# Turning the second chunk's y by VectorE blocks and placing transfers instead of TensorE transposes, in a one-core mixer kernel

## The chip, the cores and the metric

The kernel runs on one core of one Trainium2 chip. The metric is the device time of one execution in microseconds (us). Before the change it is 747.01 us, the median of 3 runs (746.77 to 747.2).

## The reference, cut to what matters

```python
def _layernorm(x, axis=-1, eps=1e-5):
    m = jnp.mean(x, axis=axis, keepdims=True)
    v = jnp.var(x, axis=axis, keepdims=True)
    return (x - m) / jnp.sqrt(v + eps)
...
    x = A_x                                   # [1, 2048, 512]
    xn = _layernorm(x, axis=-1)
    s = _A_ref(xn, A_wqkv, A_wo)              # 32 heads of 16, causal window of 256, then @ wo
    g = _silu(_B_ref(xn, B_w1, B_b1, B_w2, B_b2))
    return x + s * g
...
def _B_ref(x, w1, b1, w2, b2):                # w1 [512, 1792], w2 [1792, 512]
    y = _layernorm(x, axis=-1)
    h = _gelu(jnp.einsum("bsd,df->bsf", y, w1) + b1)
    return jnp.einsum("bsf,fd->bsd", h, w2) + b2
```

The MLP's input `y` is thus the layernorm of `xn`, itself a layernorm.

## The kernel before, in words

All products are made in three passes: each operand is split into a high part (a cast) and a low part (the rest), and high x high, high x low and low x high are summed. `split` (line 69) makes the pair: ScalarE casts the high part, VectorE subtracts it for the low part.

Tokens are worked in four chunks of 512. The attention comes first, up to about 433 us of the profiled span, with an order that is written out by hand (steps `t`, lists `plan`, `fills`, `ends`). The layernorms `xn` of the first two chunks are kept in DRAM (`xn_d`), the attention's raw outputs and the denominators of its softmax in `oT_d`.

Then the MLP and the output projection follow, chunk by chunk. The loop at line 1087 works chunk 0 (`c == 0`) and chunk 1 (`c == 1`). Its inner loop (line 1112) has 15 steps `i`; a step handles one block `f` of 128 hidden features:

- `activate(f)`: ScalarE makes the gelu `g` and the high part `gh`, VectorE the low part `gl`. `gh` and `gl` have two buffers each.
- `project(f)` of the block before it: 12 matmuls into the four accumulators `acc`, in the order high, high, low for each of them.
- `hidden(f)`: 12 matmuls `h` with the transposed `y` as moving operand. In chunk 0 only blocks 4 and 5 are made in the loop, at steps 2 and 3; the others were made during the attention and, from block 6 on, lie in DRAM (`h_d`), from where they are fetched as `hr`. The blocks are worked in the order 2, 3, 0, 1, 4, 5, 6 to 13.

Between these the loop of chunk 0 does three side jobs:

- `late_w`: the rest of the weights (`w`, `wos`) is split.
- The denominators: `fetch_sums` (step 2) loads `den` from `oT_d`; VectorE takes its reciprocal in four parts at steps 4 to 7; SyncE writes it to `rden_d`. At steps 8 to 11 `load_o` loads the attention's outputs `or` and, spread over partitions, their reciprocals `w<-rden_d`; a step later VectorE multiplies them (line 1149), and another step later `split_o` makes `ohl`, which the output projection reads.
- The second chunk's `y`: `load_y(1)` at step 4 loads four tiles of 128 tokens from `xn_d`; from step 6 to 11 VectorE makes mean and variance (`BATCH_NORM`), GpSimd the power -1/2 (`rs`), and VectorE applies them.

`end_chunk` (line 944) is the seam between two chunks: VectorE adds the bias to `acc`, ScalarE makes the silu, and for each of four tiles TensorE makes the output projection `s` (12 matmuls), VectorE multiplies it by the gate, GpSimd adds `x` (`xo`), SyncE stores. Before tiles 0 and 2 of the seam after chunk 0, `between` calls `y_transpose` twice (line 643): for each 128 features TensorE turns four 128x128 blocks of `y` into a PSUM bank `yt`, and `split` makes high and low part of the turned `y` from it (`yh`, `xnT`). After the seam chunk 1 begins with three `hidden`, which read these.

The `y` of chunks 2 and 3 goes another way already, during chunk 1: ScalarE normalises, VectorE turns each tile in square blocks of 32x32 in place (`turn_y`, line 888), SyncE stores it to `z_d`, and `fetch_y` (line 895) loads it back in four transfers for each 128 features, which put the blocks in their places.

The order on each engine is the program's order: every operation is issued through the class `Ordered` (line 32). Only SyncE, which issues all the DMAs, is left to the scheduler where `nc.sync.on` is False; in the loop it was on for chunk 1 and off for chunk 0 (line 1111). An engine works its instructions in order, so one that waits holds up all behind it on that engine.

Of the kernel before, what the change touches and what calls it, by code (L numbers as in the profile page):

```python
# [9 lines left out]
F32 = mybir.dt.float32  # L10
# [8 lines left out]
P = 128  # L19
NCH = S // 512  # L20
NKB = S // P
KT = D // P
# [28 lines left out]
def mixer_kernel(ctx, tc, x, wqk, wv, wo, w1, b1, w2, b2, out):  # L51


    nc = SimpleNamespace(**{name: Ordered(tc, name) for name in ("tensor", "vector", "scalar", "gpsimd", "sync")})
# [5 lines left out]
    dram = ctx.enter_context(tc.tile_pool(name="dram", bufs=1, space=bass.MemoryType.DRAM))  # L60
# [8 lines left out]
    def split(dst_hi, dst_lo, src, eng=None):  # L69

        (eng or nc.scalar.copy)(dst_hi, src)
        nc.vector.tensor_sub(dst_lo, src, dst_hi.bitcast(F32))
# [4 lines left out]
    def load(pool, tag, src, name, shape=(P, 512)):  # L77
        t = pool.tile(list(shape), F32, tag=tag, name=name)
        nc.sync.dma_start(t, src)
        return t  # L80
# [83 lines left out]
    def load_x(c, pools, name):  # L164
        return [load(*pools[i % len(pools)], x[512 * c + P * i: 512 * c + P * (i + 1), :], f"{name}_{c}_{i}")
                for i in range(4)]
# [15 lines left out]
    xn_d = dram.tile([8, P, D], F32, name="xn_d")  # L182
# [3 lines left out]
    w_d = {"w1": dram.tile([P, NF * 512], F32, name="w1_d"), "w2": dram.tile([P, NF * 512], F32, name="w2_d"),  # L186
           "wo": dram.tile([P, 4 * 512], F32, name="wo_d")}
    g_d = dram.tile([NF, P, 512], F32, name="g_d")
    z_d = dram.tile([2, 4, P, 512], F32, name="z_d")
    mT_d = dram.tile([NQ, NCH, 32, P], F32, name="mT_d")  # L190


# [31 lines left out]
    ident = const.tile([P, P], F32, name="ident")  # L224
# [360 lines left out]
    mlp = {}  # L585
# [34 lines left out]
    def w_part(kind, a, f):  # L620
        return {"w1": w1_part, "w2": w2_part, "wo": lambda a, f: wos[:, a, f]}[kind](a, f)
# [6 lines left out]
    def fetch(kind, f):  # L628

        nc.sync.dma_start(w_part(kind, 1, f).bitcast(F32), w_d[kind][:, 512 * f: 512 * (f + 1)])  # L630
# [9 lines left out]
    def y_steps(a, b):  # L640
        run(mlp["ln"][a:b])

    def y_transpose(c, kt, ps=None):
        ts = mlp["y"]
        if ps is None:
            ps = ps_yt.tile([P, 512], F32, tag="b", name=f"yt_{c}_{kt}")
        for i in range(4):
            nc.tensor.transpose(ps[:, P * i: P * (i + 1)], ts[i][:, P * kt: P * (kt + 1)], ident)
        split(mlp["yy"][0][kt], mlp["yy"][1][kt], ps)

    def hidden_mm(ps, f, k):
        kt, (a, b) = k // 3, PASSES[k % 3]
        nc.tensor.matmul(ps, w1_part(a, f)[:, P * kt: P * (kt + 1)], mlp["yy"][b][kt],
# [38 lines left out]
    ln = layernorm(xs[0], "A0", True, True, 3)  # L692
# [171 lines left out]
    ps_yt = ctx.enter_context(tc.tile_pool(name="ps_yt", bufs=2, space=PSUM))  # L864
# [6 lines left out]
    wos = cp.tile([P, 2, 4, 512], F32R, name="wos")  # L871
    for f in range(W2_FIRST, NF):
        fetch("w2", f)
    for f in range(6, NF, 2):
        t = gp.tile([P, 2, 512], F32, tag="ohl", name=f"hr_{f}", bufs=4)
        nc.sync.dma_start(t, h_d[f - 6: f - 4].rearrange("f p t -> p f t"))
        ready.update({f: t[:, 0], f + 1: t[:, 1]})
# [3 lines left out]
        fetch("wo", g)  # L881

    def load_y(c):
        if c > 1:
            return load_x(c, ((mlp["yp"], "y"),), "y")
        return [load(mlp["yp"], "y", xn_d[4 * c + i], f"y_{c}_{i}") for i in range(4)]

    def turn_y(c, tiles):

        for i in tiles:  # L890
            y = mlp["y"][i]
            nc.vector.transpose(y, y)
            nc.sync.dma_start(z_d[c - 2, i], y)

    def fetch_y(c, kt, dst):

        for k in range(4):
            at = z_d[c - 2, 0, 0, 128 * kt + 32 * k: 128 * kt + 32 * k + 32]
            nc.sync.dma_start(dst[32 * k: 32 * k + 32].rearrange("p (t j) -> p t j", j=32),
                              bass.AP(tensor=at.tensor, offset=at.offset, ap=[[512, 32], [32 * 512, 16], [1, 32]]))  # L900

# [185 lines left out]
    for c in range(2):  # L1087
        accs = open_accs(c)
        gs, os_, hs, wanted = {}, [], {}, []
        made = ready if c == 0 else {}  # L1090

        def hidden(f):
            hs[f] = (ps_yt if c and f % 2 else ps_st).tile([P, 512], F32, tag="b", name=f"h_{c}_{f}")
            for k in range(3 * KT):
                hidden_mm(hs[f], f, k)

        def activate(f):
            if f in made and f in soon:
                gs[f] = made[f]
                return  # L1100
            src = made[f] if f in made else hs.pop(f)
            g = src if f in made and f < 2 else t2.tile([P, 512], F32, tag="t2", name=f"g_{c}_{f}")
            nc.scalar.activation(g, src, AF.Gelu_apprx_tanh, bias=b1s[:, f: f + 1])
            gs[f] = split_g(c, f, g, nc.scalar.copy)

        order = [2, 3, 0, 1, 4, 5, *range(6, NF)] if c == 0 else [*range(NF)]
        ahead = 2 + c
        for f in range(ahead if c else 0):
            hidden(f)
        o_from, o_late = (0, 0) if c else (8, 1)  # L1110
        nc.sync.on = c > 0
        for i in range(NF + 1):
            if i < NF:
                activate(order[i])
            if c and i in (1, 2, 6, 7):
                y_steps(6, 10)
            if c and i >= 10 and i < 14:
                second_y(i - 10)
            if c and i == 14:
                kept["w"] = bigp.tile([P, 768], F32R, tag="wb1", name="wsh")  # L1120
                combine_w(0)
            if c == 0:
                for kind, f in late_w[LATE[i]: LATE[i + 1]]:
                    settle(kind, f, nc.scalar.copy, nc.vector)
            if i >= 1:
                project(accs, [(order[i - 1], gs.pop(order[i - 1]))], order[0], order[-1])
            if i + ahead < NF and order[i + ahead] not in made and order[i + ahead] > 1:
                hidden(order[i + ahead])
            if c == 0:
                if i == 2:  # L1130
                    den = fetch_sums()
                if 4 <= i < 8:
                    nc.vector.reciprocal(den[:, P * (i - 4): P * (i - 3)], den[:, P * (i - 4): P * (i - 3)])
                    if i == 7:
                        nc.sync.dma_start(rden_d.rearrange("g a (c t) -> (g a c) t", c=NCH), den)
                if i == 4:
                    mlp["y"] = load_y(1)
                if i == 6:
                    mlp["ln"] = layernorm(mlp["y"], "C1", False)
                for back, (a, b) in enumerate(((0, 2), (2, 4), (4, 5), (5, 6), (6, 8), (8, 10))):  # L1140
                    if i == 6 + min(back, 5):
                        y_steps(a, b)
            else:
                steps2(i)
            k = i - o_from
            if 0 <= k - 2 - o_late < 4:
                os_.append(split_o(c, k - 2 - o_late, wanted[k - 2 - o_late][0]))
            if 0 <= k - 1 - o_late < 4:
                nc.vector.tensor_mul(wanted[k - 1 - o_late][0], *wanted[k - 1 - o_late])
            if 0 <= k < 4:  # L1150
                wanted.append(load_o(c, k))
            if c:
                if i in (2, 3, 7, 8):
                    turn_y(2 + i // 5, (0, 1) if i in (2, 7) else (2, 3))
                if i == 3:
                    mlp["y"] = load_y(3)
                    kept[0] = gated[:, 2:4]
                    kept[1] = bigp.tile([P, 2, 512], F32, tag="wb1", name="y2_21")
                    for kt in range(KT):
                        fetch_y(2, kt, kept[kt // 2][:, kt % 2])  # L1160
                if i in (8, 9):
                    for kt in (2 * i - 16, 2 * i - 15):
                        put("21" if kt > 1 else "11", kt % 2, kept[kt // 2][:, kt % 2])
                if i == 8:
                    fetch_second()
                if i == 12:
                    fetch_pair(0)
            if c and i in (0, 1, 5, 6):
                y_steps(5, 6)
        nc.sync.on = False  # L1170
        if c == 0:
            gated = bigp.tile([P, 4, 512], F32, tag="wa", name="gated")

        def between(i):
            if c == 0 and i in (0, 2):
                y_transpose(1, i)
                y_transpose(1, i + 1)
                if i == 2:
                    mlp["y"] = load_y(2)
            if c == 1 and i in (1, 2):  # L1180
                split_w(0, 2 * i - 2)
                split_w(0, 2 * i - 1)
        end_chunk(c, accs, os_, between)
        if c == 0:
            steps2(-1)
# [148 lines left out]
```

## Time and profile before

| what | value |
|---|---|
| median of 3 runs | 747.01 us |
| the profiled execution's own time | 747.81 us |
| its span, first to last instruction | 746.1 us |
| mean granted TensorE clock | 0.998 |
| TensorE matmuls busy | 730.9 us (98%) |
| VectorE busy | 515.6 us (69%) |
| ScalarE busy | 436.9 us (59%) |
| GpSimd busy | 297.8 us (40%) |
| seam after chunk 0: first `yt` to the first `h` of chunk 1 | 476.92 to 489.58 us |

The page of the profile gives for each engine its busy time, slices of the span in tenths, the DMA queues, the chain of work that ended last, and groups of instructions. Rows of the timeline give the start, the duration, the engine, the operation with its output and inputs, how many like it follow at once, and, in square brackets, how long the engine sat idle before and what ended that. PE is TensorE's matmul, PEld its weight load, DVE VectorE, ACT ScalarE, POOL GpSimd, SPq the queue of SyncE, whose rows are the issuing of a DMA and not its transfer. All operations have line 43, the helper that records them, so they are told apart by their tiles.

### The profile page before, as it was taken

The numbers are of one execution on the slowest core, as the hardware profiler recorded it, in microseconds if no ns is written. First come the engines' busy times: TensorE is split into PE (matmuls) and PEld (weight loads), VectorE is DVE, ScalarE is ACT, GpSimd is POOL, SyncE is SP. The second block draws the span as 40 slices with busy tenths as digits, with TensorE's granted clock in tenths as the row PEclk, the third lists the DMA queues.
The fourth block names the chain that finished last, engine by engine and source line by source line (L and its number), as shares of the span: only waits on it lengthen the run. The fifth ranks groups of instructions, "written<-read, shape, count | busy, mean of one in ns | idle before, by whom it ended". The sixth has DMA issues, their size and how long they took to land.

```text
span 746.1 us, 18779 instructions
## 1 busy us (share of the span) xinstructions
PE 730.9 (98%) x7376; PEld 587.8 (79%) x7376; DVE 515.6 (69%) x789; ACT 436.9 (59%) x740; POOL 297.8 (40%) x644
## 2 busy tenths in 40 slices
PE   8999999999999999999999999999999999999997
PEld 7886777777778887777776688888888888888886
DVE  6886777877766678887773547856658755676643
ACT  7757767867667676778877745443544733442001
POOL 7313757757666555767867700030102000001102
PEclk9999999999999999999999999999999999999999
DMA  8633355667555625656725383356453322253611
GB/s 288 193 65 79 84 141 149 187 171 197 140 137 149 154 70 150 156 138 165 212 91 161 92 289 108 120 197 203 101 107 113 95 90 74 69 183 115 218 50 57
DMA packets 75001, 103.61 MB, mean 139 GB/s; under 512 B 28128, under 2 KB 28384, under 8 KB 74912
## 3 DMA queue, kind: packets, MB, share of 16 engines
q1 hardware_dynamic: 74912, 102.40, 48.4%
q8 instruction: 58, 0.95, 0.5%
q14 instruction: 31, 0.25, 0.1%
HBM read 53.48 MB, written 31.72 MB: 114 GB/s over the span
## 4 chain that ended last, share of the span: by engine, by line
PE 89%; ACT 5%; DVE 2%; POOL 2%; issue 1%; DMA 1%; SPq 0%; DVEq 0%; ACTq 0%; POOLq 0%
PE acc L43 20%; PE fb L43 19%; PE zo L43 11%; PE stb L43 9%; PE p L43 9%; PE s L43 6%; PE h L43 6%; PE xy L43 5%; ACT pt L43 4%; PE pv L43 3%; POOL pt L43 1%; DVE xy L43 1%; DMA x<-in_x_dram 1%; DVE mt L43 0%; ACT pjr L43 0%
## 5 line engine op out<-in xcount | busy, mean ns | idle before, releaser
L43 POOL TENSOR_SCALAR_AFFINE_SELECT pt<-pt 128x256 f32<-128x256 f32 x480 | 192.9, 426 | 133.8 <-ACT pt L43 131.2
L43 ACT ACTIVATE pt<-stb 128x768 f32<-128x768 f32 (+1 forms) x244 | 188.5, 773 | 62.6 <-PE stb L43 55.4
L43 DVE TENSOR_REDUCE mt<-xy 128x4 f32<-128x1024 f32 (+1 forms) x128 | 152.6, 1192 | 4.4
L43 DVE COPY_PREDICATED xy<-upper,zo 128x512 f32<-128x512 int32 x112 | 77.8, 695 | 70.5 <-PE xy L43 62.9
L43 POOL TENSOR_TENSOR xo<-xo,gated 128x512 f32<-128x512 f32 x15 | 19.9, 1330 | 218.3 <-DVE gated L43 214.2
L43 PE MATMUL fb<-xnT,wqb 64*128 64x512 f32 (+1 forms) x684 | 104.6, 397 | 0.2
L43 PE MATMUL zo<-pt,vt 128*17 128x128 f32 x2880 | 103.7, 275 | 0.3 <-POOL pt L43 0.3
L43 PE MATMUL stb<-qk 64*128 64x384 f32 (+1 forms) x488 | 97.2, 393 | 6.2 <-ACT pt L43 4.1
L43 PE MATMUL acc<-w,gh 128*128 128x512 f32 x320 | 98.6, 389 | 0.0
L43 PEld LDWEIGHTS stb<-qk 64*128 64x128 f32 x488 | 45.8, 183 | 51.6 <-ACT pt L43 46.4
L43 PEld LDWEIGHTS zo<-pt,vt 128*17 128x17 f32 x2880 | 67.5, 97 | 15.6 <-issue 6.4
L43 PEld LDWEIGHTS fb<-xnT,wqb 64*128 64x128 f32 (+1 forms) x684 | 64.6, 185 | 10.9 <-DVE pjr L43 1.4
L43 PEld LDWEIGHTS acc<-w,gh 128*128 128x128 f32 x320 | 60.1, 188 | 12.5
L43 PE MATMUL acc<-w,gl 128*128 128x512 f32 x160 | 62.4, 390 | 0.0
L43 PE MATMUL xy<-qk 64*128 64x256 f32 (+2 forms) x536 | 58.4, 291 | 0.2
L43 PEld LDWEIGHTS xy<-qk 64*128 64x128 f32 x536 | 46.7, 185 | 6.7 <-issue 3.1
L43 ACT COPY oraw<-zo 128x128 f32<-128x128 f32 x128 | 34.0, 266 | 29.4 <-PE zo L43 29.0
L43 ACT ACTIVATE gated<-acc 128x512 f32<-128x512 f32 x16 | 8.7, 595 | 63.4 <-DVE acc L43 63.4
L43 PE MATMUL s<-wos,ohl 128*128 128x512 f32 (+1 forms) x204 | 44.7, 377 | 0.0
L43 PEld LDWEIGHTS s<-wos,ohl 128*128 128x128 f32 x204 | 36.7, 188 | 7.0
L43 PEld LDWEIGHTS zo<-qk 64*128 64x128 f32 x448 | 38.6, 185 | 4.4 <-issue 1.4
L43 ACT COPY p<-p 128x512 f32<-128x512 f32 x21 | 12.3, 584 | 48.8 <-PE p L43 41.5
(193 smaller groups left out, 1235.1 us busy)
## 6 DMA issues: line engine op xcount, KB each, us to landing
qk<-sh SPq DMA_DIRECT2D x128, 128.0 KB
qk<-pjr SPq DMA_DIRECT2D x64, 128.0 KB
oT_d<-oraw SPq DMA_DIRECT2D x32, 256.0 KB
w_d<-in_w_dram SPq DMA_DIRECT2D x14, 512.0 KB
x<-in_x_dram SPq DMA_DIRECT2D x16, 256.0 KB
or<-oT_d SPq DMA_DIRECT2D x16, 256.0 KB
w<-rden_d SPq DMA_DIRECT2D x16, 256.0 KB
xo<-in_x_dram SPq DMA_DIRECT2D x16, 256.0 KB
```

The source lines that it names most:

```text
L43: r = issue(*args, **kwargs)
```

## The change

The `y` of chunk 1 goes the way of those of chunks 2 and 3. It is loaded before the loop of chunk 0, ahead of the `hr` loads; at step 3 VectorE makes its statistics, at step 4 ScalarE normalises it, VectorE turns it in blocks and SyncE stores it; at step 5 SyncE loads it back in 16 transfers of 64 KB into the places of the low parts; at steps 9 to 12 ScalarE casts the high part and VectorE subtracts it in place. The 16 transposes of TensorE and `y_transpose` are gone. The load of the third chunk's `y` moves from the seam to step 12. SyncE's order in the loop of chunk 0 is now the program's.

```diff
-    z_d = dram.tile([2, 4, P, 512], F32, name="z_d")
+    z_d = dram.tile([NCH - 1, 4, P, 512], F32, name="z_d")
...
-    def y_transpose(c, kt, ps=None):
-        ts = mlp["y"]
-        if ps is None:
-            ps = ps_yt.tile([P, 512], F32, tag="b", name=f"yt_{c}_{kt}")
-        for i in range(4):
-            nc.tensor.transpose(ps[:, P * i: P * (i + 1)], ts[i][:, P * kt: P * (kt + 1)], ident)
-        split(mlp["yy"][0][kt], mlp["yy"][1][kt], ps)
...
     for f in range(W2_FIRST, NF):
         fetch("w2", f)
+    mlp["y"] = [load(mlp["yp"], "y", xn_d[4 + i], f"y_1_{i}") for i in range(4)]
     for f in range(6, NF, 2):
         t = gp.tile([P, 2, 512], F32, tag="ohl", name=f"hr_{f}", bufs=4)
         nc.sync.dma_start(t, h_d[f - 6: f - 4].rearrange("f p t -> p f t"))
...
-            nc.sync.dma_start(z_d[c - 2, i], y)
+            nc.sync.dma_start(z_d[c - 1, i], y)
...
-            at = z_d[c - 2, 0, 0, 128 * kt + 32 * k: 128 * kt + 32 * k + 32]
+            at = z_d[c - 1, 0, 0, 128 * kt + 32 * k: 128 * kt + 32 * k + 32]
...
-        nc.sync.on = c > 0
+        nc.sync.on = True
...
             if c == 0:
                 if i == 2:
                     den = fetch_sums()
                 if 4 <= i < 8:
                     nc.vector.reciprocal(den[:, P * (i - 4): P * (i - 3)], den[:, P * (i - 4): P * (i - 3)])
                     if i == 7:
                         nc.sync.dma_start(rden_d.rearrange("g a (c t) -> (g a c) t", c=NCH), den)
+                if i == 3:
+                    mlp["ln"] = layernorm(mlp["y"], "C1", True)
+                    y_steps(0, 5)
                 if i == 4:
-                    mlp["y"] = load_y(1)
-                if i == 6:
-                    mlp["ln"] = layernorm(mlp["y"], "C1", False)
-                for back, (a, b) in enumerate(((0, 2), (2, 4), (4, 5), (5, 6), (6, 8), (8, 10))):
-                    if i == 6 + min(back, 5):
-                        y_steps(a, b)
+                    y_steps(5, 10)
+                    turn_y(1, range(4))
+                if i == 5:
+                    for kt in range(KT):
+                        fetch_y(1, kt, mlp["yy"][1][kt].bitcast(F32))
+                if 9 <= i < 13:
+                    split(mlp["yy"][0][i - 9], mlp["yy"][1][i - 9], mlp["yy"][1][i - 9].bitcast(F32))
+                if i == 12:
+                    mlp["y"] = load_y(2)
...
         def between(i):
-            if c == 0 and i in (0, 2):
-                y_transpose(1, i)
-                y_transpose(1, i + 1)
-                if i == 2:
-                    mlp["y"] = load_y(2)
```

Here `y_steps(0, 5)` is four statistics and the power on GpSimd, `y_steps(5, 10)` the shift (a small operation of VectorE) and four normalisations, which run on ScalarE since the third argument of `layernorm` is now True. At step 4 these stand in the program behind the first reciprocal of `den`. The stores of `turn_y` and the 16 loads of `fetch_y` stand in SyncE's order ahead of the store of the reciprocals to `rden_d` (step 7) and of the loads of `load_o` (from step 8).

More of the change, by code (lines that the diff above doesn't have):

```diff
@@ L883, in load_y @@
     def load_y(c):
-        if c > 1:
-            return load_x(c, ((mlp["yp"], "y"),), "y")
-        return [load(mlp["yp"], "y", xn_d[4 * c + i], f"y_{c}_{i}") for i in range(4)]
+        return load_x(c, ((mlp["yp"], "y"),), "y")
     def turn_y(c, tiles):
```

## The prediction

> **What bounds the kernel now.** I read the page's busy times first, then the chain of waits from 446 to 490 us, where the change lies, then the busy time of that stretch.
>
> ```profile
> PE 730.9 (98%) x7376; PEld 587.8 (79%) x7376; DVE 515.6 (69%) x789; ACT 436.9 (59%) x740; POOL 297.8 (40%) x644
> ```
>
> ```profile
> 446.90 30.18 PE acc L43 x132
> 477.08 0.87 PE yt L43 x8
> 477.95 5.46 PE s L43 x24
> 483.41 0.87 PE yt L43 x8
> 484.29 5.46 PE s L43 x24
> ```
>
> ```profile
> 426.00:489.74 63.74, 63.74 (x329) 52.13 (x318) 41.13 (x71) 32.21 (x53) 5.63 (x5) 1.00 0.56 179
> ```
>
> TensorE has no gap at all from 426 to 489.74 us, at a granted clock of 1.00: in this stretch its own work sets the end, and VectorE (41.13 of 63.74 us) and ScalarE (32.21) lie beside it. So whatever leaves TensorE is gained, and whatever makes it wait is lost in full.
>
> **What the change removes.** The 16 transposes are two pieces of 0.87 us on the chain: **-1.74 us**. Their casts and subtractions at the seam go to steps 9 to 12, where ScalarE and VectorE have room:
>
> ```profile
> 460.35 0.62 ACT L43 CAST gh<-g 128x512 fp32r<-128x512 f32 x1 [0.95 <-ACT g L43]
> ```
>
> I cost them at nothing while the loads of step 5 are in time. This is the cast of step 9 (block 9), some 466 after the first wait below; the first four loads are issued by 461.3 in the count below. If they came late, ScalarE would stand, and block 10 behind it.
>
> **The first wait that it adds.** At step 4 VectorE takes the first reciprocal of `den`, and only then makes the shift; ScalarE's four normalisations need the shift, and stand ahead of the gelu and cast of block 5.
>
> ```profile
> 446.93 0.69 ACT L43 ACTIVATE g<-h,b1s 128x512 f32<-128x512 f32 x1 [1.76 <-PE h L43]
> 449.47 0.62 ACT L43 CAST gh<-g 128x512 fp32r<-128x512 f32 x1 [1.85 <-PE acc L43]
> ...
> 449.21 0.95 DVE L43 RECIPROCAL den<-den 128x128 f32<-128x128 f32 x1 [3.24 <-DMA den<-oT_d]
> ...
> 451.95 0.41 PEld L43 LDWEIGHTS acc<-w,gh 128*128 128x128 f32 x2
> 452.40 0.19 PEld L43 LDWEIGHTS acc<-w,gl 128*128 128x128 f32 x1
> ...
> 434.50:444.00 9.50, 9.50 (x43) 7.88 (x42) 4.46 (x7) 5.21 (x9) 0.00 (x0) 1.00 1.01 349
> 444.00:449.20 5.20, 5.20 (x24) 4.32 (x23) 1.29 (x2) 1.83 (x3) 0.00 (x0) 1.00 0.65 219
> ...
> 445.44 2.22 SPq L43 DMA_DIRECT2D y<-xn_d  x4
> ```
>
> Block 5's cast ends at 449.47 + 0.62 = 450.09 and TensorE loads it at 451.95: 1.86 us to spare. But the reciprocal starts at 449.21, because `den` lands then. And `den` will land later: the four loads of `y` (256 KB each, 1.05 MB) were issued behind it, at 445.44, and are now ahead of it, in a stretch where the DMA engines are full (share 1.01, 349 GB/s). 1.05 MB at 349 GB/s are 3.0 us. Its ends: 0, if the loads find room, and 4.8 at the 219 GB/s of the stretch from 444 us on. I take 3.0, since the loads sit ahead of the full stretch and not in the room behind it: `den` lands at D = 452.2.
>
> What follows the reciprocal, with durations from the same operations at other places:
>
> ```profile
> 457.67 0.95 DVE L43 RECIPROCAL den<-den 128x128 f32<-128x128 f32 x1
> 458.54 0.64 DVE L43 BATCH_NORM_STATS2 bnC<-y 128x6 f32<-128x512 f32 x1
> ...
> 531.55 0.16 DVE L43 SCALAR_TENSOR_TENSOR shiftC<-mvC,rsC 128x4 f32<-128x4 f32 x1 [1.21 <-POOL rsC L43]
> 532.60 1.42 DVE L43 STREAM_TRANSPOSE y<-y 128x512 f32<-128x512 f32 x2 [0.28 <-ACT y L43]
> ...
> 531.75 2.93 ACT L43 ACTIVATE y<-y,shiftC,rsC 128x512 f32<-128x512 f32 x4 [0.72 <-DVE shiftC L43]
> 534.59 0.66 ACT L43 ACTIVATE g<-h,b1s 128x512 f32<-128x512 f32 x1
> ...
> 492.50 0.69 ACT L43 ACTIVATE g<-h,b1s 128x512 f32<-128x512 f32 x1 [6.24 <-PE h L43]
> 493.22 0.62 ACT L43 CAST gh<-g 128x512 fp32r<-128x512 f32 x1
> ```
>
> Reciprocal to the next operation 458.54 - 457.67 = 0.87; shift to the first normalisation 0.20; from there to the gelu 534.59 - 531.75 = 2.84; gelu to cast 0.72; cast 0.62: together 5.25. Block 5's cast ends at 452.2 + 5.25 = 457.45 instead of before 451.95, so TensorE stands for 5.5 us. The low part takes 0.04 + 0.69 more, where TensorE reads it 0.45 behind the high part: 0.28 more. **First wait: 5.8 us** (2.8 with D as it was, 7.6 with 4.8). The statistics themselves are no part of it: VectorE idled 4.67 us ahead of block 4's low part at 444.69, and four of 0.64 us with their small aggregates fit in.
>
> ```profile
> 444.69 0.69 DVE L43 TENSOR_TENSOR gl<-g,gh 128x512 fp32r<-128x512 f32 x1 [4.67 <-ACT gh L43]
> ```
>
> **The second wait.** SyncE's queue is now in the program's order: four stores to `z_d`, which wait for the transposes, 16 loads, which wait for the stores to land, and only then the store of the reciprocals and the loads of `or` and `w`.
>
> ```profile
> 537.11 1.30 DVE L43 STREAM_TRANSPOSE y<-y 128x512 f32<-128x512 f32 x2
> 537.84 0.91 SPq L43 DMA_DIRECT2D z_d<-y  x2
> 540.61 8.42 SPq L43 DMA_DIRECT2D xnT<-z_d  x16
> ...
> 458.65 0.32 SPq L43 DMA_DIRECT2D rden_d<-den  x1
> 460.63 1.19 SPq L43 DMA_DIRECT2D w<-rden_d  x2
> ...
> 467.25 0.69 DVE L43 TENSOR_TENSOR or<-or,w 128x512 f32<-128x512 f32 x1 [1.73 <-DMA w<-rden_d]
> 467.87 0.68 DVE L43 TENSOR_TENSOR gl<-g,gh 128x512 fp32r<-128x512 f32 x1
> 470.44 0.69 DVE L43 TENSOR_TENSOR or<-or,w 128x512 f32<-128x512 f32 x1
> 472.71 0.68 DVE L43 TENSOR_TENSOR or<-or,w 128x512 f32<-128x512 f32 x1
> ...
> 468.90 0.19 PEld L43 LDWEIGHTS acc<-w,gl 128*128 128x128 f32 x1
> ```
>
> The fourth normalisation ends at D + 0.87 + 0.20 + 2.93 = 456.2, the fourth transpose 0.75 later at 456.95 (1.42 for two). From the end of the transposes (537.11 + 1.30 = 538.41) to the first load (540.61) are 2.20, the 16 loads take 8.42: SyncE is free at 467.6. The reciprocals are long done, so their store goes out at 467.6 and not at 458.65. From that store to the first product `or` x `w` were 467.25 - 458.65 = 8.60 us: it comes at 476.2. Behind it on VectorE stands block 11's low part, which ended 467.87 + 0.68 - 467.25 = 1.30 after: 477.5. TensorE read that at 468.90 (it was hardly in time before), now at 468.90 + 5.8 = 474.7. **Second wait: 2.8 us**, whatever D is, since both sides move with it. Its ends: 0, and 4.3 if the loads from `z_d` are issued as slowly as eight of them were in chunk 1 (4.94 us), so 1.5 more:
>
> ```profile
> 522.45 4.94 SPq L43 DMA_DIRECT2D y<-z_d  x8
> ```
>
> The next products followed after 3.19 and 2.27 us (467.25, 470.44, 472.71), TensorE's step is 12 x 0.227 = 2.72 (30.18 us for 132 matmuls): **0.5 us** for 3.19 - 2.72, between 0 and 2, since one load of `or` more now stands between the first two `w`. The last `ohl` was done 9.6 us after the first product, so at some 486 to 487, and the output projection, due at 477.95 + 9.1 - 0.87 = 486.2, needs it with its tenth matmul, 2 us in: no third wait. The load of `y` for the third chunk goes out earlier and costs nothing.
>
> One place where the Trainium skill would have it otherwise: "DMA: Bandwidth & Descriptors", section "Anatomy of one DMA", gives a transfer some 2.0 us plus its bytes over 436 GB/s, an estimate of 2.6 us for the 256 KB of a `w`. The row says 467.25 - 460.63 = 6.6. By the page the first `w` would come 4 us earlier and the second wait would be gone, which is the second rival below; I go by the row.
>
> **Sum.** 5.8 + 2.8 + 0.5 - 1.74 = +7.4 us. The profiled execution took 747.81 us around its span of 746.1, so it would take 755.2; the median before is 0.8 below it, and the forecast for the median is 747.0 + 7.4 = **754.4 us**.
>
> **The rivals.**
>
> 1. The loads of `y` fit beside the others and `den` lands at 449.2 as before. For it speaks the room at 432 to 434.5 us (a share of 0.65 below), against it the full share right behind. First wait 2.8: 747.0 + 2.8 + 2.8 + 0.5 - 1.74 = 751.4.
>
> ```profile
> 432.00:434.50 2.50, 2.50 (x13) 2.06 (x12) 0.43 (x2) 1.17 (x3) 0.00 (x0) 1.00 0.65 147
> ```
>
> 2. The first wait as forecast, but `w` lands as soon as another transfer of 256 KB did: the four stores to `z_d` took 2.20 us until the load that waits for them. Then `or` x `w` comes at 467.6 + 2.0 + 2.2 = 471.8, and neither of the later waits is left: 747.0 + 5.8 - 1.74 = 751.1. Against it stands the 6.6 us.
>
> 3. All upper ends together: 7.6 + 4.3 + 2 - 1.74 = +12, 759.
>
> 4. **Faster.** The chain from `den` is short enough and only the removed transposes count: 747.0 - 1.74 = 745.3. The place is VectorE's first reciprocal. With D up to 446.6 block 5 is in time (446.6 + 5.25 = 451.9); block 11's low part, at D + 25.3, is in time up to D = 468.9 - 25.3 = 443.6. Between these the wait eats the gain, which is even at D = 445.3: earlier is faster, later slower. `den` landed at 449.21, and nothing that was ahead of it has gone from its queue; so I give it little. A part of it is that the change does what it says without harm, because the shift doesn't wait for the reciprocal; the program's order says that it does.
>
> **How the numbers follow.** Forecast 0.58; `den` as before 0.14; `w` quickly there 0.12; the upper ends 0.06; faster 0.06; a mixture that comes out even 0.04. A measurement of this kernel can tell about 0.2%, 1.5 us, from no change. Slower by more than that: 0.90; within: 0.04; faster: 0.06. The range for 8 in 10 runs from 750.0 to 757.0: it holds the forecast with most of its ends and both cases near 751.
>
> **What would show it.** After the change the chain of waits should leave TensorE twice in this stretch: once near 452 us, through gelu and cast of block 5, the normalisations, the reciprocal and `den`, with some 5.5 us of idle time at TensorE; once near 475, through a low part, `or` and `w<-rden_d`, for some 3. The first reciprocal should start near 452 and the store to `rden_d` near 467.6. If the reciprocal starts by 445, or the shift ahead of it, the first step is wrong; if the store to `rden_d` stands ahead of the 16 loads, the second. The seam should be 1.74 us shorter, from the first `s` to the first `h` of chunk 1 with no `yt` between; if TensorE waits there, the covers that I costed at nothing are gone.

## The result, and the profile after

The changed kernel takes **753.81 us** (median of 4 runs, 753.44 to 754.40) beside 746.98 us before (4 runs): a ratio of 1.0092, with a 95% interval of 1.0075 to 1.011. It is 6.8 us slower; the forecast was 754.4. The profiled execution took 753.44 us around a span of 751.7. The busy times of the page:

```profile
PE 731.5 (97%) x7360; PEld 587.0 (78%) x7360; DVE 516.9 (69%) x790; ACT 439.8 (59%) x744; POOL 297.7 (40%) x644
```

TensorE has 16 instructions less and 0.6 us more busy time: it did less and did part of it slower. The chain of waits (start, length, what) says where:

```profile
446.31 3.82 DMA den<-oT_d
...
450.25 0.95 DVE den L43
...
451.98 2.21 ACT y L43 x3
454.18 0.58 ACT g L43
...
454.79 0.63 ACT gh L43
...
455.46 12.86 PE acc L43 x47
...
470.32 10.39 DMA w<-rden_d
...
481.35 0.69 DVE gl L43
...
482.08 2.56 PE acc L43 x10
484.65 10.88 PE s L43 x48
495.53 9.52 PE h L43 x42
```

Before, this stretch was TensorE from end to end. Now the chain leaves it twice. The first time it goes back through cast, gelu, normalisations and reciprocal to the landing of `den`; the second time through a low part and a product to `w<-rden_d`. That is the third of the four products, at block 13: its `w` was issued at 470.32 and landed 10.39 us later. The wait at the first product, which the prediction has in mind, is not on this chain; by the chain, TensorE would have waited for the third `w` without it too. From 484.65 us `s` runs 10.88 us without a `yt` between: before, from the first `yt` to the first `h`, it was 484.29 + 5.46 - 477.08 = 12.67. The seam is 1.79 shorter.

The first wait in the timeline (start, length, engine, what; in brackets the idle time before it and what ended it):

```profile
450.25 0.95 DVE L43 RECIPROCAL den<-den 128x128 f32<-128x128 f32 x1 [5.14 <-DMA den<-oT_d]
451.12 0.10 DVE L43 SCALAR_TENSOR_TENSOR shiftC<-mvC,rsC 128x4 f32<-128x4 f32 x1
451.26 2.93 ACT L43 ACTIVATE y<-y,shiftC,rsC 128x512 f32<-128x512 f32 x4 [6.96 <-DVE shiftC L43]
455.46 0.30 PEld L43 LDWEIGHTS acc<-w,gh 128*128 128x128 f32 x2 [4.42 <-ACT gh L43]
456.18 0.19 PEld L43 LDWEIGHTS acc<-w,gl 128*128 128x128 f32 x1 [0.43 <-DVE gl L43]
...
457.33 0.76 PEld L43 LDWEIGHTS acc<-w,gh 128*128 128x128 f32 x2
...
459.89 0.46 PEld L43 LDWEIGHTS acc<-w,gh 128*128 128x128 f32 x2
```

ScalarE stands 6.96 us for a shift of 0.10 us, which stands behind a reciprocal that waits for its transfer. TensorE stands 4.42 us. Then come two weight loads in 0.76 us, which take 0.41 elsewhere. Block 5 has 12 loads: it begins at 455.46, block 6 at 459.89, so it takes 4.43 us instead of 2.72. The busy times by stretch (busy us of PE, PEld, DVE, ACT and POOL, then the granted clock, the DMA share and GB/s) show what was slow:

```profile
446.00:451.00 5.00, 5.00 (x24) 4.14 (x23) 0.76 (x1) 0.00 (x0) 0.00 (x0) 1.00 0.27 99
451.00:455.40 4.40, 0.46 (x3) 0.04 (x1) 3.04 (x6) 4.11 (x7) 0.00 (x0) 1.00 0.38 146
455.40:460.00 4.60, 4.54 (x12) 3.33 (x13) 4.16 (x6) 2.91 (x6) 0.00 (x0) 0.63 0.53 136
460.00:465.00 5.00, 5.00 (x24) 4.10 (x23) 3.45 (x5) 3.54 (x6) 0.00 (x0) 1.00 0.80 126
```

TensorE's clock was 0.63 for the 4.6 us behind the idle time, and 1.00 around them; asked in slices of 0.4 us, it was 0.50 from 456.6 to 459.8 us. The prediction has no such term. That the idle time is the cause is what e3 and e12 test below.

The second wait, first in SyncE's queue, then at VectorE and TensorE:

```profile
457.12 8.29 SPq L43 DMA_DIRECT2D xnT<-z_d  x16
465.50 0.43 SPq L43 DMA_DIRECT2D rden_d<-den  x1
...
467.77 0.60 SPq L43 DMA_DIRECT2D w<-rden_d  x1
...
474.11 3.48 SPq L43 DMA_DIRECT2D y<-in_x_dram  x4
...
474.20 0.69 DVE L43 TENSOR_TENSOR or<-or,w 128x512 f32<-128x512 f32 x1 [3.86 <-DMA w<-rden_d]
...
475.55 0.19 PEld L43 LDWEIGHTS acc<-w,gl 128*128 128x128 f32 x1 [1.55 <-DVE gl L43]
...
478.42 0.19 PEld L43 LDWEIGHTS acc<-w,gl 128*128 128x128 f32 x1 [0.24 <-DVE gl L43]
...
482.08 0.19 PEld L43 LDWEIGHTS acc<-w,gl 128*128 128x128 f32 x1 [1.07 <-DVE gl L43]
```

The store goes out when the 16 loads are issued, the first product comes 8.70 us behind it, and three low parts are late.

How much all this is, from the first load of the last `h` block (which is ahead of everything that the change touches) to the first load of the seam, before and after:

```profile
443.79 0.19 PEld L43 LDWEIGHTS h<-yh,w 128*128 128x128 f32 x1
...
476.69 1.02 PEld L43 LDWEIGHTS yt<-ident,y 128*128 128x128 f32 x8
```

```profile
442.91 0.19 PEld L43 LDWEIGHTS h<-yh,w 128*128 128x128 f32 x1
...
484.26 10.84 PEld L43 LDWEIGHTS s<-wos,ohl 128*128 128x128 f32 x48
```

32.90 us have become 41.35: 8.45 more, less 1.79 at the seam is +6.66, and the medians differ by 6.83. A block's 12 loads take 2.72 us where nothing holds them up; in the changed kernel block 5 takes 4.43, block 11 4.18, block 12 2.83 and block 13 3.67. The two profiles are shifted by 0.88 us against each other (443.79 and 442.91), so times of different kernels are compared below by what lies between two events, not as they stand.

### The profile page after: what moved, and what is told of

Read it like the earlier page. It is cut to its first block, busy times and chain, and to the rows that moved or that the text cites. A ratio compares the mean times of both kernels' runs of the same rounds, so it can differ in the third digit from the quotient of the medians.

```text
span 751.7 us, 18804 instructions
## 1 busy us (share of the span) xinstructions
PE 731.5 (97%) x7360; PEld 587.0 (78%) x7360; DVE 516.9 (69%) x790; ACT 439.8 (59%) x744; POOL 297.7 (40%) x644
## 4 chain that ended last, share of the span: by engine, by line
PE 83%; DMA 6%; ACT 5%; DVE 3%; issue 2%; POOL 2%; SPq 1%; DVEq 0%; ACTq 0%; POOLq 0%
PE fb L43 17%; PE acc L43 17%; PE zo L43 11%; PE p L43 9%; PE stb L43 9%; PE s L43 6%; PE h L43 5%; PE xy L43 5%; ACT pt L43 4%; PE pv L43 3%; DMA w<-rden_d 1%; POOL pt L43 1%; DMA b2s<-in_b_dram 1%; DMA y<-xn_d 1%; DVE xy L43 1%
```

## The experiments

The theory: three causes lie in a row. The shift stands behind the reciprocal of `den` on VectorE; TensorE loses its clock by the idle time; the store to `rden_d` stands behind the 16 loads on SyncE. Rivals: the later waits come from the DMA engines' share and not from the queue; the slow matmuls from something else than the idle time.

| kernel | median us (runs) | ratio to before, 95% |
|---|---|---|
| the change | 753.81 (4) | 1.0075 to 1.011 |
| e1 shift first | 750.02 (5) | 1.003 to 1.0055 |
| e2 loads from z_d late | 757.12 (4) | 1.0124 to 1.0155 |
| e3 the same, wait filled | 756.51 (4) | 1.0115 to 1.0143 |
| e4 shift first, loads in two parts | 751.93 (5) | 1.0054 to 1.008 |
| e5 store and w apart | 753.46 (4) | 1.0071 to 1.0099 |
| e6 shift first, store and w apart | 748.55 (11) | 1.0015 to 1.004 |
| e7 as e5, wait filled | 754.67 (5) | 1.0083 to 1.012 |
| e8 before, y loaded early | 748.07 (11) | 1.0005 to 1.0023 |
| e9 third chunk's y late | 753.01 (4) | 1.0069 to 1.0097 |
| e10 as e5, third chunk's y late | 751.34 (5) | 1.0049 to 1.0074 |
| e11 as e6, third chunk's y late | 749.73 (7) | 1.0022 to 1.0043 |
| e12 as e10, wait filled | 749.92 (5) | 1.0027 to 1.0054 |

The kernel before was at 746.82 to 746.96 beside all of them. No variant is faster than it.

### e1: the shift ahead of the reciprocal

```
+                if i == 4:
+                    y_steps(5, 10)
+                    turn_y(1, range(4))
                 if 4 <= i < 8:
                     nc.vector.reciprocal(...)
...
-                if i == 4:
-                    y_steps(5, 10)
-                    turn_y(1, range(4))
```

> The changed kernel, with the shift, the four normalisations and the four square transposes of step 4 ahead of the first reciprocal of den on VectorE. Theory (the shift stands behind the reciprocal, and the store to rden_d behind the 16 loads): the shift starts near 445.2 instead of 451.12, block 5's cast ends by 450, TensorE has no idle 4.4 us and keeps its full clock behind it; 0.4 us are left because the low part of block 5 still stands behind the reciprocal. The 16 loads are issued from some 451.2 to 459.6, so the store to rden_d goes out near 459.6 (465.50 after the change), the first product of or and w near 468.2, block 11's low part ends near 469.5 and is due near 468.0: a second wait of 1.5, a third of 0.6. Sum of the waits 2.5 instead of 8.4: 753.8 - 5.9 = 747.9 us. Rival 1 (the normalisations themselves, 2.93 us ahead of block 5's gelu, are too late for block 5 whatever they wait for): the first wait stays in part, 2 us or more, 750 or above. Rival 2 (the later waits are not set by SyncE's queue): they vanish with the first wait, 745.6.

Measured 750.02. The first wait is gone but for a low part, as the theory says; what is left is the second. Timeline of e1, SyncE, VectorE and TensorE, and then its stretch from 470 us:

```profile
447.62 2.15 SPq L43 DMA_DIRECT2D z_d<-y  x4
453.40 8.29 SPq L43 DMA_DIRECT2D xnT<-z_d  x16
461.79 0.43 SPq L43 DMA_DIRECT2D rden_d<-den  x1
...
470.28 0.69 DVE L43 TENSOR_TENSOR or<-or,w 128x512 f32<-128x512 f32 x1 [5.38 <-DMA w<-rden_d]
...
471.63 0.19 PEld L43 LDWEIGHTS acc<-w,gl 128*128 128x128 f32 x1 [3.07 <-DVE gl L43]
```

```profile
470.00:475.00 5.00, 3.37 (x10) 2.71 (x11) 4.69 (x9) 2.49 (x4) 0.00 (x0) 0.77 0.72 199
```

The second wait grew from 1.55 to 3.07, and the clock fell to 0.77 behind it. Without the first wait block 11 came 5.7 us earlier (24.93 us behind the first load of the last `h` block instead of 30.67), and the first product only 4.2 (27.07 instead of 31.29). The expectation was 2.1 too low: the loads from `z_d` began 4.2 us behind the last transpose (449.19 to 453.40) and not 2.2, and the lost clock was again not in it.

### e2: the loads from z_d behind those of or and w

```
-                if i == 5:
-                    for kt in range(KT):
-                        fetch_y(1, kt, ...)
-                if 9 <= i < 13:
+                if 11 <= i < 15:
                     split(...)
...
                 wanted.append(load_o(c, k))
+                if c == 0:
+                    fetch_y(1, k, mlp["yy"][1][k].bitcast(F32))
```

> The changed kernel, with the 16 loads from z_d taken out of step 5 and put, four at a time, behind the or and w loads of steps 8 to 11; the casts go from steps 9 to 12 to steps 11 to 14. Theory (the second and third wait come from the store to rden_d standing behind the 16 loads on SyncE): the store goes out near 462, when the fourth reciprocal is done, instead of 465.50; the first product comes near 470.6, ahead of what TensorE needs; the waits of 1.55, 0.24 and 1.07 us near 475 to 482 go and those near 451 to 460 stay: 753.8 - 2.3 = 751.5 us. Rival (the loads of w are late by themselves, since they share the DMA engines with whatever SyncE issues beside them): the waits stay, 753 to 754.

Measured 757.12, a miss to the other side. The first product was in time, but the pieces of `y` and the later `w`, issued in turn, now came late: ScalarE's cast and VectorE's subtraction of a piece waited for its load, and the low part or the `ohl` behind it with them. TensorE in e2:

```profile
482.27 0.19 PEld L43 LDWEIGHTS acc<-w,gl 128*128 128x128 f32 x1 [2.50 <-DVE gl L43]
488.73 0.30 PEld L43 LDWEIGHTS s<-wos,ohl 128*128 128x128 f32 x2 [2.28 <-DVE ohl L43]
```

So this kernel doesn't tell the question. It shows the price of a cover: the casts that the prediction put at nothing "while the loads of step 5 are in time" cost several us when they are not.

### e3: 16 idle matmuls in the first wait

```
+            if c == 0 and i == 6:
+                fill = ps_st.tile([P, 512], F32, tag="b", name="fill")
+                for k in range(16):
+                    nc.tensor.matmul(fill, w2_part(1, 4)[:, 0:P], w2_part(0, 4), ...)
```

> The kernel with the loads from z_d late, and besides 16 matmuls of 128x512 on weights that are there already, into a bank that nothing reads, ahead of block 5's product: they fill 3.6 of the 4.4 us in which TensorE stands and add nothing to the output. Theory (the slow matmuls behind the idle time, at a granted clock of 0.63 from 455.4 to 460 us, come from the idle time itself): the clock stays at 1.00 there, block 5 takes 2.7 us instead of 4.4, and the time is 1.7 below that of the kernel without the 16 matmuls: 749.8 us. Rival (they are slow from something else that happens then, the weights' or ScalarE's traffic): the clock or the durations of block 5 stay as they are and the time is the same, 751.5 or a little more.

Measured 756.51, no clear difference to e2. The trace tells more than the time. The stretch behind the first wait in e2, and then in e3:

```profile
455.40:460.00 4.60, 4.17 (x10) 3.07 (x11) 4.16 (x6) 3.29 (x6) 0.00 (x0) 0.64 0.30 116
```

```profile
455.40:460.00 4.60, 4.45 (x18) 3.39 (x19) 4.47 (x7) 4.30 (x9) 0.00 (x0) 1.00 0.25 96
```

With TensorE busy in the wait the clock stays at 1.00, and the two kernels differ by nothing but the 16 matmuls. Block 5 took 2.92 us instead of 4.48. What was so gained went into later waits for the pieces of `y` and for `w`: blocks 12 and 13 took 9.61 us instead of 7.81.

### e4: shift first, the loads from z_d in two parts

```
                 if i == 5:
-                    for kt in range(KT):
+                    for kt in range(2):
                         fetch_y(1, kt, ...)
...
                 wanted.append(load_o(c, k))
+                if c == 0 and k in (1, 2):
+                    fetch_y(1, k + 1, ...)
```

> The shift, normalisations and transposes ahead of the reciprocal, and of the 16 loads from z_d only eight at step 5, the others four at a time behind the or and w loads of steps 9 and 10, with the casts at steps 11 to 14. Theory (two queues alone make the loss: VectorE's behind den and SyncE's behind the loads): the store to rden_d goes out near 458 as before the change, no later wait is left, 0.4 us of the first, and the removed transposes count: 747.0 - 1.74 + 0.4 = 745.7 us, faster than both kernels. Rival (the added transfers and VectorE's transposes cost something by themselves beside the other work): 747 or above.

Measured 751.93, worse than e1. The store to `rden_d` went out behind eight loads instead of 16, and the first two products were in time; but the last `or` and `w` now stood behind the second part, the last product waited 4.89 us for a `w` issued 8.2 us ahead of it (473.84 to 482.02), and the output projection for `ohl`:

```profile
482.02 0.69 DVE L43 TENSOR_TENSOR or<-or,w 128x512 f32<-128x512 f32 x1 [4.89 <-DMA w<-rden_d]
...
483.70 0.30 PEld L43 LDWEIGHTS s<-wos,ohl 128*128 128x128 f32 x2 [4.00 <-DVE ohl L43]
```

### e5, e9 and e10: the queue, or the DMA engines

In e5 the store of the reciprocals and the `or` and `w` loads of this chunk are issued by GpSimd. In e9 only the third chunk's loads of `y` are put back into the output projection. e10 is both.

```
-                        nc.sync.dma_start(rden_d.rearrange(...), den)
+                        nc.gpsimd.dma_start(rden_d.rearrange(...), den)
...
+        q = nc.sync if c else nc.gpsimd
...
-        nc.sync.dma_start(rec, ...)
+        q.dma_start(rec, ...)
```

```
-                if i == 12:
-                    mlp["y"] = load_y(2)
...
         def between(i):
+            if c == 0 and i == 2:
+                ...
+                    nc.gpsimd.dma_start(mlp["y"][k], x[1024 + P * k: 1152 + P * k, :])
```

> The changed kernel, with the store to rden_d and the or and w loads of steps 8 to 11 issued by GpSimd, which has no work there, instead of by SyncE; nothing is moved in time on the other engines. In the kernel with late loads from z_d the casts of y came too late and made waits of their own, so that it did not tell the question. Theory (the waits near 475 to 482 come from the store standing behind the 16 loads in SyncE's queue): the store goes out near 461.5, when the fourth reciprocal is done, the first product of or and w comes near 470, and those waits go while the first and the half clock behind it stay: 753.8 - 2.3 = 751.5 us. Rival (w is late by its own landing, or by the 16 loads' share of the DMA engines): the first product stays near 474 and the time near 753.8.

> The changed kernel, with only the four loads of y for the third chunk (256 KB each) put back into the output projection, where the kernel before had them (issued by GpSimd behind the second token block, so that they cannot be issued early). The prediction put their earlier place at nothing. Theory (the last two w loads share the DMA engines with them: 0.74 to 0.96 of them busy from 475 to 485 us): the waits of 0.24 and 1.07 us at block 12 and 13 shrink and the time falls by some 1 us to 752.8. Rival (w is late from SyncE's queue alone): 753.8.

> The store to rden_d and the or and w loads of steps 8 to 11 issued by GpSimd, and the third chunk's y loads back in the output projection. In the kernel without the second part the store went out 2 us earlier, but w did not land earlier: the y loads had moved up with the free queue and filled the DMA engines (share 1.06 from 470 to 475 us). Theory (the second wait is SyncE's queue plus the DMA engines' share; both are now as before): first product of or and w near 470.5, no wait behind the first, 753.8 - 2.6 = 751.2 us. Rival (the 16 loads in pieces of 128 bytes are enough to hold w up): first product near 473 or later, 752.5 to 754.

e5: 753.46, as the change. The store went out 2 us earlier, and `w` landed no earlier:

```profile
463.54 0.83 POOL L43 DMA_DIRECT2D rden_d<-den  x1 [19.94 <-DMA xnT<-z_d]
...
474.84 0.69 DVE L43 TENSOR_TENSOR or<-or,w 128x512 f32<-128x512 f32 x1 [4.23 <-DMA w<-rden_d]
...
470.00:475.00 5.00, 4.69 (x21) 3.56 (x19) 0.77 (x3) 1.57 (x3) 1.18 (x2) 1.00 1.06 283
```

From store to product were 11.3 us instead of 8.7, with the DMA engines full (share 1.06). SyncE, free early, had sent the third chunk's `y` at once, ahead of `w` in the engines. The Trainium skill says in "DMA: Bandwidth & Descriptors", section "Issuing engines are not separate DMA queues", that transfers of all issuing engines share the same 16 DMA engines and that a second issuer saves only issue time; the share of 1.06 agrees.

e9: 753.01, 0.8 below the change; the runs of the two don't overlap, though the intervals of their ratios do. The waits at blocks 11 to 13 are 1.25, 0.28 and 0.46 (1.55, 0.24, 1.07). e10: 751.34, as expected: the first product 8.7 us behind its store again, at 471.82, and no wait at block 11. The wait at block 11 is therefore the queue's, as long as the third chunk's `y` is not ahead of `w` in the DMA engines; and the earlier load of `y`, which the prediction put at nothing, costs some 0.8 us. The wait at block 13 is not the queue's: e10 still has 1.17 us there, with the DMA engines full (share 1.05 from 475 to 480 us).

### e7 and e12: the price of the clock

e7 is e5 with the 16 matmuls of e3, e12 is e10 with them.

> The kernel with the store and the or and w loads on GpSimd, shift behind the reciprocal as in the changed kernel, and 16 matmuls into a bank that nothing reads ahead of block 5's product; they add nothing to the output. Theory (the clock of 0.63 behind the first wait comes from the idle time, and costs 1.7 us): 1.7 us below the kernel without the 16 matmuls: 749.8 us. Rival (the lost 1.7 us are hidden in a later wait anyway): the same as without them.

> As the kernel with the store apart and the y loads late, with the shift behind the reciprocal as in the changed kernel, and 16 matmuls into a bank that nothing reads in the first wait; they add nothing to the output. In the two earlier pairs the clock stayed at 1.00 with them, but later waits hid what it gained. Theory (the half clock behind the first wait costs 1.7 us): 1.7 below the kernel without them, 749.5 if that one is at 751.2. Rival (the gain goes into the wait for w again): the same as without them.

e7: 754.67, with runs from 752.36 to 756.32, so no clear difference to e5. The clock was 1.00 up to 480 us, but the third `w` landed late in full DMA engines and TensorE stood 4.00 us in block 13: the gain went into that wait. e12 against e10 is the pair in which it was kept: 749.92 beside 751.34, 1.42 us less. Not all of this is the clock. In the two profiles block 5 takes 2.91 us instead of 4.00, **1.1 us**; 0.7 more is that blocks 11 to 13 waited less. The same stretch, in e10 and in e12:

```profile
455.40:460.00 4.60, 4.22 (x12) 3.36 (x13) 4.16 (x6) 3.23 (x6) 0.00 (x0) 0.64 0.57 157
```

```profile
455.40:460.00 4.60, 4.38 (x18) 3.34 (x19) 4.40 (x7) 4.32 (x9) 0.00 (x0) 1.00 0.56 148
```

The price differs from kernel to kernel: behind nearly the same wait block 5 took 4.00 us in e10, 4.43 in the change and 4.86 in e5, against 2.91 or 2.92 with the wait filled.

### e8: the kernel before, with y loaded early

```
     for f in range(W2_FIRST, NF):
         fetch("w2", f)
+    mlp["y"] = [load(mlp["yp"], "y", xn_d[4 + i], f"y_1_{i}") for i in range(4)]
...
-                if i == 4:
-                    mlp["y"] = load_y(1)
```

> The kernel before the change, with only its four loads of y for the second chunk moved to the place where the changed kernel has them, ahead of the hr loads. Theory (den lands later since 1.05 MB are now ahead of it on SyncE and the DMA engines): the first reciprocal starts 1.9 us later, near 451.1 instead of 449.21, and since nothing waits behind it there, the time stays at 747.0 within 0.5 us. Rival (den is later for another reason, the changed order of the rest of SyncE's queue): the reciprocal stays near 449.2.

The first reciprocal started at 450.56. In this profile the chain's last `acc` ahead of it starts at 446.22 (446.90 before), so that is 451.24 in the times of before: 2.0 us later than 449.21, by the `y` loads alone. The time is 748.07, 1.1 above before, where none was expected. VectorE's later reciprocals and statistics now stand ahead of the low parts:

```profile
450.56 0.95 DVE L43 RECIPROCAL den<-den 128x128 f32<-128x128 f32 x1 [5.26 <-DMA den<-oT_d]
...
461.35 0.19 PEld L43 LDWEIGHTS acc<-w,gl 128*128 128x128 f32 x1 [1.01 <-DVE gl L43]
```

### e6 and e11: all causes taken away

e6 is e1 with store, `or` and `w` on GpSimd as in e5; e11 has besides the third chunk's `y` late as in e9.

> Shift, normalisations and transposes ahead of the reciprocal, and besides the store to rden_d and the or and w loads issued by GpSimd. Theory (two queues make the whole loss, and each alone leaves the other's part): the first wait is gone as in the kernel with the shift first alone, the store goes out near 457.8 instead of 461.79, the first product near 466.5 instead of 470.28, in time; 0.4 us are left for the low part of block 5, and the removed transposes count: 747.0 - 1.74 + 0.4 = 745.7 us. Rival 1 (w takes longer beside the 16 loads than before the change): a second wait of 1 to 3 us is left, 747 to 749. Rival 2 (GpSimd's issues are slow): the first product near 470 and 750.

> All three: shift ahead of the reciprocal, store and or and w loads on GpSimd, the third chunk's y loads back in the output projection. Theory (VectorE's queue, SyncE's queue and the DMA engines' share of the moved y loads make the whole loss): no waits but 0.2 at block 5, 747.0 - 1.74 + 0.3 = 745.5 us, faster than both kernels. Rival (the 16 loads themselves hold up the second and third w): waits of 1 to 2 us left near 470 to 480, 746.5 to 748.

e6: 748.55 (runs from 747.78 to 753.22), e11: 749.73 (748.19 to 750.31); 2.9 and 4.2 us above what the theory said, and no run below those of the kernel before. The two are not told apart by these runs. The first wait is gone, and the first product is so early in both that VectorE idles 2.12 and 2.44 us ahead of it and block 11 is in time. What is left is in e11 this:

```profile
472.86 0.62 ACT L43 CAST xnT<-xnT 128x512 fp32r<-128x512 f32 x1 [3.53 <-DMA xnT<-z_d]
...
474.80 0.30 PEld L43 LDWEIGHTS acc<-w,gh 128*128 128x128 f32 x2 [1.71 <-ACT gh L43]
...
465.00:470.00 5.00, 5.00 (x24) 4.07 (x23) 3.31 (x6) 2.43 (x4) 0.05 (x1) 1.00 1.06 173
```

The DMA engines are full (share 1.06) and move 173 GB/s. The pieces of `y` and the `w` loads are now on their way at the same time: a piece lands late, ScalarE's cast of it, which idles 3.53 us for it, stands ahead of block 13's gelu, and TensorE waits behind that. In e6 such a piece is late as well (its cast idles 2.43 us for it, and TensorE 1.74 for block 13's low part), and then the last `w`. So the rival that gave the later waits to the DMA engines holds for these kernels: freed of both queues, they wait for transfers. That the 16 loads are what fills the engines is likely but not shown: no run leaves them out. How many us they cost by themselves, with everything else in the best place, was not found.

## Why the prediction was right

**The first wait** was right in its place and its chain. From the reciprocal's start to the end of block 5's cast were 454.79 + 0.62 - 450.25 = 5.16 us (5.25 in the prediction). The mis-sized term is D: the reciprocal was 450.25 + 0.88 = 451.13 in the times of before, 1.9 later than 449.21 and not 3.0; e8 gives 2.0 for the loads alone. In the rows of SyncE's queue it ended issuing `den` 2.4 us later (446.95 + 0.88 instead of 445.40), and the reciprocal followed 3.3 us behind that instead of 3.8. So D did not follow the 1.05 MB over 349 GB/s; how much of the 2.4 us is SyncE's queue and how much the engines behind it was not tested apart. TensorE stood 4.4 us, not 5.5. The low part behind it cost 0.2 (block 5 took 2.91 instead of 2.72 us at full clock), about as said.

**What it missed** is what the wait does to TensorE: 4.43 - 2.91 = 1.5 us at a lower clock. The prediction took a wait to cost its own length. That the first wait still comes out near its forecast, 4.4 + 0.2 + 1.5 = 6.1 against 5.8, is luck: two errors nearly cancel.

**The second wait** was right in its mechanism: store behind the loads, product 8.70 us behind the store (8.60). Its size was 1.5 and not 2.8 (block 11 took 4.18 instead of 2.72 us), since TensorE had lost 1.5 us of clock by then and needed block 11's low part that much later. "Whatever D is, since both sides move with it" held for the product's side: it came 474.20 - 450.25 = 23.95 us behind the reciprocal, 24.0 in the prediction. It did not hold for TensorE's side, which also moves with the clock lost behind the wait. No run moves D alone in the changed kernel.

**The third** was 1.0 to 1.1 instead of 0.5: the next products followed after 2.88 and 3.66 us (474.20, 477.08, 480.74) and not after 3.19 and 2.27, and blocks 12 and 13 took 0.1 and 0.95 more than 2.72. The earlier load of the third chunk's `y`, put at nothing, can account for the difference: without it (e9) the wait at block 13 is 0.46 instead of 1.07. This is the wait at which the chain leaves TensorE for the last time.

**What left** was right: 1.79 at the seam for 1.74, and no wait there. The casts at steps 9 to 12 cost nothing, as said, since their loads were in time; e2 and e11 show what they cost otherwise.

**The rivals.** `den` did not land as before. A quick `w` did not come: 474.20 - 467.77 = 6.4 us, at a DMA share of 0.59 and below, so the row was right and the 2.6 us of the Trainium skill were not. The section fits its figure to transfers that GpSimd issues, but with GpSimd issuing, in e10, it was 471.82 - 466.16 = 5.7 us. Faster needed `den` earlier, or a shift that doesn't wait for it; e1 gives it the second and is still slower than before, since the store to `rden_d` stays behind the loads.

Sum: 4.4 + 0.2 + 1.5 + 1.5 + 1.0 = 8.6 for the 9.1 of the prediction; the 8.45 of the traces is lower because blocks 8 and 12 took 2.90 and 2.80 us before too. From both go 1.8 and 1.74 at the seam. The total came out within 0.6 us partly because a missing term stood against terms that were too large.

## What to carry to other kernels

A step moved earlier inherits what its engine's queue is waiting for at the new place: look for the instruction that idles longest there, and put the step ahead of it. Behind each wait of TensorE of several us, expect a second loss from its clock (1.1 to 1.9 us here, behind waits of 4.3 to 4.5 us); and where several waits follow one another, removing the first shows the next in full. A second issuing engine frees a queue, not the DMA engines: transfers that had been held back now compete.

## What the runs showed of the hardware

- **The clock behind idle time.** After 4.4 us of idle time the granted clock was 0.63 over the next 4.6 us, and 1.00 with matmuls in the wait (e3, e12). Followed in slices of 0.4 us, it was 0.50 for about 3.4 us in the change (456.6 to 460.0) and in e10 (455.3 to 458.8), where it began in the idle time already, so that block 5 lost less; in e5 it was 0.50 for about 6.8 us (453.5 to 460.3). After 1.55 us there was no loss. Near 3.1 us it went both ways: e1 lost clock after 3.07 us (0.77), e3 kept it after 3.06 ahead of the output projection:

```profile
489.45 0.30 PEld L43 LDWEIGHTS s<-wos,ohl 128*128 128x128 f32 x2 [3.06 <-DVE ohl L43]
...
490.00:495.00 5.00, 4.95 (x21) 3.66 (x21) 4.01 (x7) 3.23 (x5) 1.53 (x2) 1.00 0.66 244
```

 The Trainium skill, "TensorE: Matmul & The Clock Gate", section "Part 1: The HAM clock gate", has the clock halved after a window of some 3.4 us without work, in windows that run freely. The trace agrees on the length: a mean of 0.63 over 4.6 us is 3.4 us at half clock (an estimate: 0.37 x 4.6 / 0.5), and e5's 6.8 us are twice that. It does not agree on the condition: e1 lost its clock after 3.07 us of idle time, less than such a window, and e11 (0.50 from 476.2 to 479.4 us) after two waits of 1.71 and 1.43 us with two weight loads between them.
- **Pieces of 128 bytes.** From 460 to 465 us of the changed kernel mostly the 16 loads from `z_d` are under way: 126 GB/s at a share of 0.80, thus some 158 GB/s for full engines, where the loads of before reached 349 GB/s at 1.01. Their 1.05 MB take 6.6 us of all 16 engines (estimates from these rows). That the small pieces are the reason was not tested by themselves.
